# A new order for all engines in a windowed-attention and feed-forward kernel

## The chip, the cores and the metric

The kernel runs on one core of one Trainium2 chip. The metric is the device time of one execution in microseconds (us). Before the change it is 201.78 us, the median of 3 runs (201.47 to 201.82).

## What is computed

```
scores = q @ k.T / 8 - slope[h] * distance          # 4 batches, 8 heads, 768 positions, head size 64
keep   = (key < 8) | (0 <= query - key < 96)        # 8 global keys and a window of 96
a      = softmax(where(keep, scores, -1e9))
x      = (a @ v) laid out as 3072 tokens x 512
h      = x @ w_in                                   # 512 x 2048
out    = (h - tanh(h)) @ w_out                      # 2048 x 512, float32
```

## The kernel before

The 3072 tokens are cut into 24 blocks of 128 (numbered u = 0 to 23; blocks 0 to 3 are the first of each batch). A block needs only its own keys, those of the block before it, and the 8 global keys, which stand in the first block of its batch. Everything runs in one program without loops on the chip: the text `ORDER` lists some 970 steps by name, and at its end the kernel walks through the list and issues each step on its engine (lines 799 to 806). An engine executes its own steps in this order and waits, where a step needs another engine's result or a buffer that is still read; so the list is the schedule. `/a`, `/d`, `/p`, `/s` behind a name choose ScalarE (ACT), VectorE (DVE), GpSimd (POOL) or SyncE (SP) for a step that more than one engine can do. A second text, `HOMES`, says for each tile which buffer or PSUM bank it lives in; a wait for a free buffer comes from there.

The steps by name, with their lines in the profile:

- `lq.u`, `lk.u`, `lv.u` load a block's queries, keys and values (128 KB each as bfloat16). From block 4 on they are DMAs that POOL issues (L342), cast on the way; `in.j` and `out.j` (L345, L348) load the two weight matrices the same way.
- `T.u` transposes queries and keys. For blocks 0 to 6 the matrix engine (PE) does it, and `Te` copies the result out of PSUM; from block 7 on `T.u` is one DMA transpose that SP issues (L377). `K.u` and `V.u` copy the 8 global keys and values in.
- `S.n` computes scores on PE (L396), `E.u.o` the exponential on ACT (L403), `M` multiplies by the mask on DVE (L407, L412), `AV.u` multiplies by the values on PE (L427), `R` and `N` divide (L433, L444; L440 if ACT divides).
- `X.u` and `Xe.u` bring the block into transposed form; from block 8 on `Xe.u` is a DMA transpose on SP (L466).
- `m1.g.f` multiplies a group of blocks by pieces of w_in on PE (L477), `th` takes tanh on ACT (L576), `g` the difference on DVE (L590). Groups 0 and 1 are single blocks, 2 to 6 pairs, 7 to 9 fours. In groups 8 and 9 most of this is done by Strassen's scheme (`v`, `y`, `d`, `e`, `q`; L536 on PE).
- The second product is done in pairs of blocks by Strassen's scheme: `w` and `n` are sums on DVE (L617, L630), `p1` to `p7` the products on PE (L645), `a0` to `a2` copies and `c11` to `c22` the results (L274, L276, L659). `st` stores a block, issued by POOL or SP (L662).

Line 274 is the helper that copies on ACT, line 276 the one that copies on DVE. The steps that matter most below are these two, of which every line is as it was:

```
    def load_natural(e, dst, src, u):
        eng(e).dma_start(out=dst, in_=rows_of(src, u).rearrange("h p d -> p h d"))
...
    def a_DT(u):
        nc.sync.dma_start_transpose(
            out=buf(("qk", u)).rearrange("p a b f -> p (a b) f"), in_=buf(("kq", u)).rearrange("p a f -> p (a f)")
        )
```

and the walk through the list is

```
        for word in ORDER.split():
...
            name, _, side = word.partition("/")
            e, fn = acts[name]
            fn({"a": ACT, "d": DVE, "p": POOL, "s": SP}[side] if e is None else e)
```

Of the kernel before, what the change touches and what calls it, by code (L numbers as in the profile page):

```python
# [42 lines left out]
AV.13 K.15/d lq.18 n2.8/d a0.8/a m1.6.14 E.14.1 c11.8 lv.15 v2.3 m1.6.4 R.13 K.14/d th.6.14 N.13/d lv.16 p6.8 g.6.14
Xe.13 th.6.4 lq.19 g.6.4 S.13 a1.8/a M.14 p5.8 E.15.1 n4.8/d m1.6.0 E.16.0 T.18 M.15 m1.6.12 a2.8/a th.6.0 T.17 m1.6.8
E.16.1 g.6.0 AV.14 n3.8/d th.6.12 Xe.12 m1.6.10 th.6.8 V.14/d R.14 g.6.12 K.16/a AV.15 g.6.8 m1.6.2 N.14/d p7.8 R.15
th.6.2 N.15/d th.6.10 m1.6.6 c22.8 Xe.15 g.6.2 p4.8 th.6.6 g.6.10 Xe.14 g.6.6 p3.8 c21.8 p1.10 n1.10/d st.9.0/p c12.8/a
T.19 v1.2 lv.17 S.14 n2.10/d a0.10/a V.15/a M.16 lq.20 p2.10 E.17.1 lq.23 p6.10 n4.10/d E.18.0 lv.19 AV.16 a1.10/d
# [795 lines left out]
```

## Time and profile before

| what | value |
|---|---|
| median of 3 runs | 201.78 us |
| span of the profiled execution, first to last instruction | 199.8 us |
| median less span: what lies around the span | 1.98 us |
| PE busy | 193.1 us (97%) |
| DVE busy | 178.6 us (89%) |
| ACT busy | 135.1 us (68%) |
| POOL busy (it issues DMAs) | 75.3 us (38%) |

The span is that of one execution under the profiler; no separate time of that execution is given, so its own time is taken as its span and the 1.98 us around it. The page's second part cuts the span into 40 slices of 5 us and gives the busy share of each engine in tenths, the granted clock of PE, and the mean busy share of the 16 DMA engines. The queries used are the timeline (instructions of one engine in order of time: start, duration, line, what it wrote from what, and in brackets the idle time before it and what ended that), the groups of instructions by line, and the DMA issues (how many, their size, and the median time from issue to landing).

### The profile page before, as it was taken

What the parts mean: (1) busy time and instruction counts of PE and PEld (TensorE: products, weight loads), DVE (VectorE), ACT (ScalarE), POOL (GpSimd) and SP (SyncE); (2) the same over time, 40 slices, a digit from 0 to 9 for tenths busy, and PEclk for the clock granted to TensorE, in tenths of its full rate; (3) what the DMA queues carried; (4) which work ended last, traced back from release to release, by engine and by line L of the source; (5) the groups of instructions that cost most, each with busy time, mean ns of one, the idle gap of its engine ahead of it and who ended that gap; (6) DMA issues with size and microseconds to landing.
All of it is one profiled execution on the core that took longest, in us unless ns stands there. A gap on an engine that the chain in (4) does not pass through costs nothing.

```text
span 199.8 us, 5524 instructions
## 1 busy us (share of the span) xinstructions
PE 193.1 (97%) x2219; PEld 157.8 (79%) x2219; DVE 178.6 (89%) x348; ACT 135.1 (68%) x234; POOL 75.3 (38%) x97
## 2 busy tenths in 40 slices
PE   8799999999999999999999999999999999999992
...
PEclk9999999999999999999999999999999999999999
DMA  5999999999999999989996998994733101001233
GB/s 148 211 180 185 198 163 207 201 156 141 193 167 196 178 153 135 133 188 171 137 158 146 140 173 192 154 155 85 55 108 121 66 0 54 3 0 52 107 132 131
DMA packets 103545, 27.36 MB, mean 137 GB/s; under 512 B 93920, under 2 KB 101472, under 8 KB 103520
## 3 DMA queue, kind: packets, MB, share of 16 engines
q0 software_dynamic: 74048, 16.78, 89.5%
...
## 4 chain that ended last, share of the span: by engine, by line
PE 85%; DVE 7%; DMA 3%; ACT 2%; issue 1%; ACTq 0%; DVEq 0%
PE ps L645 36%; PE ps L477 27%; PE ps L536 9%; PE ps L396 5%; PE ps L427 5%; DMA f<-in_q_dram 3%; DVE gall L590 2%; DVE x L444 2%; DVE mem L407 1%; PE ps L455 1%; ACT mem L403 1%; PE ps L320 1%; ACT mem L274 1%; PE ps L365 1%; ACT th L576 1%
## 5 line engine op out<-in xcount | busy, mean ns | idle before, releaser
L477 PE MATMUL ps<-xT,w_in_bf 128*128 128x256 bf16 (+2 forms) x544 | 69.0, 279 | 0.0
L477 PEld LDWEIGHTS <-w_in_bf 128*128 128x128 bf16 x544 | 47.2, 98 | 12.4
L576 ACT ACTIVATE th<-ps 128x512 f32<-128x512 f32 (+1 forms) x74 | 41.8, 591 | 18.7 <-PE ps L477 13.6
L590 DVE TENSOR_TENSOR gall<-ps,th 128x512 bf16<-128x512 f32 (+1 forms) x74 | 47.4, 668 | 6.0 <-ACT th L576 5.6
L645 PEld LDWEIGHTS <-gall 128*128 128x128 bf16 x488 | 46.4, 98 | 7.0
L662 POOL DMA_DIRECT2D out_dram<-ot x14 | 8.1, 580 | 102.5 <-ACT ot L274 52.4
L403 ACT ACTIVATE mem<-ps 128x1024 bf16<-128x1024 f32 x44 | 43.3, 1024 | 4.3 <-PE ps L396 4.2
L645 PE MATMUL ps<-w_out_bf,gall 128*128 128x256 bf16 (+1 forms) x296 | 36.3, 270 | 0.0
L274 ACT COPY sn<-ps 128x256 f32<-128x256 f32 x32 | 12.0, 375 | 20.3 <-PE ps L645 16.3
L645 PE MATMUL ps<-f,ss 128*128 128x256 bf16 x192 | 24.9, 273 | 0.0
L645 PE MATMUL ps<-wc,gall 128*128 128x256 bf16 x192 | 24.9, 273 | 0.0
L342 POOL DMA_DIRECT2D vb<-in_v_dram x24 | 21.5, 900 | 2.2 <-issue 1.0
L645 PEld LDWEIGHTS <-ss 128*128 128x128 bf16 x192 | 18.3, 98 | 2.8
L342 POOL DMA_DIRECT2D mem<-in_k_dram x20 | 17.9, 899 | 4.8 <-DMA w_out_bf<-in_moe_w_out_dram 3.1
L342 POOL DMA_DIRECT2D mem<-in_q_dram x20 | 18.1, 904 | 3.8 <-DMA w_out_bf<-in_moe_w_out_dram 3.0
L412 DVE TENSOR_TENSOR mem<-mem,mk 128x2048 bf16<-128x2048 bf16 x16 | 19.2, 1215 | 0.0
L659 DVE TENSOR_TENSOR ot<-ps,sn 128x256 f32<-128x256 f32 x36 | 14.7, 415 | 3.6 <-ACT sn L274 2.5
L444 DVE TENSOR_TENSOR x<-ps,rden 128x512 bf16<-128x512 f32 x23 | 15.8, 687 | 0.5
L274 ACT COPY mem<-ps 128x512 f32<-128x512 f32 (+1 forms) x22 | 12.7, 585 | 5.1 <-PE ps L536 3.9
L427 PEld LDWEIGHTS <-mem 128*128 128x128 bf16 x352 | 13.4, 97 | 2.1 <-ACT mem L403 0.5
L427 PE MATMUL ps<-vb,mem 128*128 128x65 bf16 x352 | 14.7, 193 | 0.0
L396 PE MATMUL ps<-mem 64*128 64x128 bf16 x352 | 13.1, 217 | 0.0
...
## 6 DMA issues: line engine op xcount, KB each, us to landing
out_dram<-ot POOLq DMA_DIRECT2D x14, 256.0 KB, 2.8
vb<-in_v_dram POOLq DMA_DIRECT2D x24, 128.0 KB, 6.2
mem<-in_q_dram POOLq DMA_DIRECT2D x22, 128.0 KB, 6.3
mem<-in_k_dram POOLq DMA_DIRECT2D x22, 128.0 KB, 6.1
out_dram<-ot SPq DMA_DIRECT2D x9, 256.0 KB, 2.0
w_out_bf<-in_moe_w_out_dram POOLq DMA_DIRECT2D x4, 512.0 KB, 10.7
w_in_bf<-in_moe_w_in_dram POOLq DMA_DIRECT2D x4, 256.0 KB, 7.6
w_in_bf<-in_moe_w_in_dram POOLq DMA_DIRECT2D x2, 512.0 KB, 11.0
```

The source lines that it names most:

```text
L274: nc.scalar.copy(out=out, in_=in_)
L342: eng(e).dma_start(out=dst, in_=rows_of(src, u).rearrange("h p d -> p h d"))
L396: nc.tensor.matmul(bank(("s", u, o), hh)[:, p * P : (p + 1) * P], buf(("qk", back[u] if o else u))[r, 1, p, :], buf(("qk", u))[r, 0, p, :] ...
L403: nc.scalar.activation(d, banks(("s", u, o), 0, 1), AF.Exp, bias=0.0, scale=scale)
L412: nc.vector.tensor_tensor(out=t, in0=t, in1=mk[:, 1:3], op=ALU.mult)
L427: nc.tensor.matmul(t[:, h // (H // 2), h % (H // 2), :], buf(("p", u, o))[:, slot(h), :], buf(("v", back[u] if o else u))[:, h, 0 : Dh + 1 ...
L444: nc.vector.tensor_tensor(out=buf(("x", u)).rearrange("q (a h) d -> q a h d", a=2), in0=t[:, :, :, 0:Dh], in1=rden.to_broadcast([P, 2, H / ...
L477: nc.tensor.matmul(t[:, (f - f0) * n : (f - f0 + 1) * n], w_in_bf[j][:, c, fo : fo + P], x[:, c, 0:n], start=(c == 0), stop=(c == CD - 1),)
L536: nc.tensor.matmul(t[:, r * 2 * P : (r + 1) * 2 * P], w(r)[:, c], x[:, c], start=first and r + c == 0, stop=c == 1, skip_group_check=not f ...
L576: nc.scalar.activation(h_view(buf(("th", g, f0)), g, m), h_view(bank(("h", g, f0)), g, m), AF.Tanh, bias=0.0, scale=1.0)
L590: nc.vector.tensor_tensor(out=o, in0=v(h), in1=v(th), op=ALU.subtract)
L645: nc.tensor.matmul(bank((holder, a))[:, c0:c1], s(f), t(f)[:, c0:c1], start=first and f == 0, stop=f == HF - 1, skip_group_check=not first,)
```

## The change

Every step is kept. The order of the list, the engine of 49 copies, divisions and stores, and nearly all places in `HOMES` are replaced; no function is changed. Per engine, PE's steps keep their number and shape. Of the steps that several engines can do, 2 more of the 24 divisions (`N`) and one half of the last `c12` go to ACT, one `c12`, 3 of the 36 copies `a` and 3 of the 16 copies `K` go to DVE, and 3 stores go from POOL to SP (net). The loads keep their engine, but POOL issues them in another order: up to `out.3` the order is as before, past it it isn't, and SP's transposes stand in another order from T.11 on.

The lists, cut to the opening, the stretch from `out.3` to `AV.10`, and the end:

```
-lq.1 lk.1 zero rel ones.0 zero:7 dist lq.2 lq.0 lk.0 zero:7 zero:7 table lq.3 turn zero:7 first zero:7 lk.3 ident slopes
-zero:7 zero:7 lk.2 ones.1 B.0 lv.1 cq.1/a ck.1/d bm.1 lv.0 T.1.1 em.1 lv.2 T.1.0 Te.1.1/d B.1 cq.0/a lv.3 Te.1.0/d
-ck.0/a T.0.0 S.1 in.0 Te.0.0/a T.3.0 B.2 E.1.0 in.1 Te.3.0/d T.0.1 Te.0.1/d in.3 T.2.1 T.3.1 Te.2.1/a T.2.0 Te.3.1/d S.0
-lq.4 Te.2.0/a AV.1 E.0.0 S.2 R.1 N.1/d in.2 B.3 E.2.0 lk.4 AV.0 S.3 R.0 N.0/d X.1 in.4 E.3.0 AV.2 Xe.1/d X.0 in.5 R.2
-N.2/d bm.2 Xe.0/a AV.3 m1.1.0 lk.5 em.2 R.3 N.3/d X.2 m1.0.0 th.1.0 Xe.2/d X.3 lq.5 th.0.0 g.1.0 m1.0.2 Xe.3/a g.0.0
...
-th.1.8 M.4.0 E.4.1 m1.0.8 g.1.8 th.2.8 out.0 M.4.1 m1.0.12 th.0.8 g.2.4 out.2 T.5.1 g.2.8 T.5.0 Te.5.1/a m1.1.12 out.3
-Te.5.0/d th.0.12 g.0.8 S.5 lk.7 th.1.12 g.0.12 AV.4 E.5.0 g.1.12 lq.7 m1.2.12 n1.0/d E.5.1 lk.10 m1.2.10 M.5.0 lq.10
-V.4/a R.4 m1.2.14 M.5.1 th.2.10 K.5/d N.4/d AV.5 th.2.14 T.6.1 X.4 R.5 Te.6.1/a T.6.0 N.5/d lq.9 Xe.4/a Te.6.0/d X.5 S.6
-Xe.5/d g.2.14 m1.3.2 E.6.1 n3.0/d m1.3.10 g.2.10 lq.8 th.2.12 w1.1 th.3.2 p1.0 E.6.0 w1.0 m1.3.12 g.2.12 a0.0/a g.3.2
-m1.3.4 lk.8 th.3.12 n2.0/d K.6/a th.3.10 m1.3.0 w2.0 m1.3.8 w4.0 w2.1 lk.9 p2.0 M.6.0 p6.0 lv.7 g.3.12 w3.1 T.7 m1.3.6
-lv.6 a1.0/a c11.0 th.3.0 w3.0 p5.0 g.3.10 p7.0 a2.0/a n1.2/d th.3.4 g.3.0 p1.2 th.3.6 n2.2/d p2.2 a0.2/a w4.1 th.3.8
-c22.0 p6.2 V.5/a n4.2/d T.8 p4.0 n3.2/d a1.2/a g.3.8 T.9 p5.2 g.3.6 p7.2 c21.0 a2.2/a T.10 g.3.4 st.1.0/p p3.2 M.6.1
-lk.11 c11.2 S.7 c12.2/a c22.2 lv.11 n4.0/d AV.6 E.7.1 p4.2 lk.12 R.6 N.6/d E.7.0 m1.3.14 lv.9 K.7/d V.6/d M.7.1 X.6
-lk.16 th.3.14 p3.0 M.7.0 Xe.6/a c21.2 lq.11 AV.7 g.3.14 c12.0/a lk.13 R.7 S.8 N.7/d lq.12 n1.4/d X.7 E.8.1 p1.4 Xe.7/d
-lv.10 n2.4/d m1.4.8 K.9/a E.8.0 v1.1 st.2.0/p n3.4/d m1.4.10 th.4.8 a0.4/d lv.8 g.4.8 p6.4 th.4.10 v2.1 E.9.0 lq.13
-m1.4.14 g.4.10 M.8 a1.4/a S.9 th.4.14 T.11 p5.4 g.4.14 E.9.1 V.7/d p2.4 a2.4/d E.10.0 M.9 T.12 m1.4.2 E.10.1 n4.4/d
-m1.4.6 K.10/a st.0.0/s M.10 AV.9 th.4.6 m1.4.0 th.4.2 g.4.6 m1.4.4 R.9 T.13 N.9/d p7.4 g.4.2 th.4.4 Xe.9 th.4.0 g.4.4
-AV.8 V.9/a p3.4 c11.4 c22.4 R.8 m1.4.12 N.8/d c12.4/a st.4.0/p g.4.0 p4.4 Xe.8 th.4.12 lq.15 v3.1 S.10 c21.4 lk.15
-g.4.12 p1.6 E.12.0 lv.13 n1.6/d p2.6 n2.6/d a0.6/a lq.14 E.11.1 K.12/d AV.10 lk.14 p6.6 E.11.0 R.10 c11.6 V.10/d lq.16
...
-c11.18 a2.20/a st.19.0/s n2.22/d c12.18/a p1.22 st.18.0/s c22.20 c11.20 p4.20 a0.22/a c11.22 p6.22 n4.22/d st.22.0/s
-c21.20 p7.22 a1.22/a st.21.0/p p5.22 p3.20 a2.22/a c22.22 p3.22.0 c12.20/a p4.22 st.20.0/s c12.22.0/d st.22.256/s
-p3.22.1 c21.22 c12.22.1/d st.23.0/s st.22.384/s
...
+lq.1 lk.1 zero rel ones.0 zero:7 dist lq.2 lq.0 lk.0 zero:7 zero:7 table lq.3 turn zero:7 first zero:7 lk.3 ident
+slopes zero:7 zero:7 lk.2 ones.1 B.0 lv.1 cq.1/a ck.1/d bm.1 lv.0 T.1.1 em.1 lv.2 T.1.0 Te.1.1/d B.1 cq.0/a T.2.0 lv.3
+Te.1.0/d ck.0/a T.0.0 S.1 in.0 T.0.1 Te.0.0/a T.3.0 Te.2.0/d T.3.1 in.1 Te.0.1/d T.2.1 S.0 Te.2.1/d E.1.0 B.2 S.2 AV.1
+in.3 Te.3.1/a E.0.0 AV.0 Te.3.0/a R.1 E.2.0 R.0 N.1/d B.3 S.3 AV.2 X.1 lq.4 in.2 N.0/d lk.4 in.4 R.2 N.2/d X.0 Xe.1/d
+bm.2 E.3.0 AV.3 X.2 Xe.0/a m1.0.0 m1.1.0 em.2 R.3 N.3/d X.3 m1.0.2 m1.1.2 th.0.0 Xe.3/a Xe.2/d in.5 lk.5 m1.2.2 th.2.2
...
+Te.5.1/a S.5 th.0.12 g.0.12 g.1.8 out.3 m1.2.14 lk.8 th.1.12 g.1.12 AV.4 m1.2.10 E.5.1 T.6.1 M.5.1 T.6.0 E.5.0 R.4
+M.5.0 lq.7 lq.8 V.4/a AV.5 N.4/d X.4 Te.6.1/a th.2.10 m1.2.12 R.5 K.5/d Te.6.0/a N.5/d X.5 Xe.4/a S.6 n1.0/d Xe.5/d
+m1.3.2 th.2.14 g.2.14 th.2.12 E.6.0 m1.3.8 m1.3.10 m1.3.6 lk.7 T.7 g.2.12 w1.1 g.2.10 th.3.2 g.3.2 V.5/a n3.0/d n1.2/d
+m1.3.0 th.3.6 E.6.1 w3.0 p1.2 a0.2/a p1.0 a0.0/a m1.3.4 n2.2/d th.3.4 p2.0 w1.0 w2.0 w2.1 w4.1 p6.2 n2.0/d p6.0 th.3.10
+a1.2/a p5.2 a1.0/a M.6.1 T.8 g.3.6 g.3.10 w3.1 c11.0 g.3.4 p2.2 n4.2/d c11.2 p7.0 p5.0 th.3.8 a2.2/a lq.9 lv.9 th.3.0
+K.6/a p3.2 m1.3.12 a2.0/a w4.0 g.3.8 c22.0 th.3.12 c12.2/a lv.6 lk.9 T.9 p4.0 n3.2/d g.3.0 p7.2 M.6.0 AV.6 V.6/a g.3.12
+c21.0 S.7 lk.10 E.7.0 c22.2 p4.2 R.6 N.6/d m1.3.14 X.6 lq.10 T.10 E.7.1 K.7/d n4.0/d p3.0 c21.2 M.7.0 lv.20 lv.7 M.7.1
+AV.7 lk.12 lk.14 th.3.14 g.3.14 Xe.6/a c12.0/a S.8 lq.19 st.1.0/p R.7 N.7/d V.7/a lk.13 X.7 p1.4 lq.12 Xe.7/d n1.4/d
+n2.4/d a0.4/d E.8.1 E.9.0 m1.4.14 E.8.0 T.12 th.4.14 g.4.14 m1.4.10 th.4.10 K.9/d g.4.10 m1.4.8 th.4.8 p6.4 a1.4/a S.9
+E.9.1 g.4.8 M.8 E.10.0 lv.8 p5.4 M.9 a2.4/a m1.4.6 th.4.6 E.10.1 lk.11 lq.11 AV.8 m1.4.12 n3.4/d th.4.12 m1.4.4 T.11
+R.8 N.8/d g.4.6 v1.2 AV.9 R.9 th.4.4 g.4.4 g.4.12 lk.16 st.0.0/p st.2.0/s v2.1 lv.14 Xe.8 st.3.0/p p2.4 c11.4 m1.4.2
+N.9/a Xe.9 m1.4.0 lv.11 n4.4/d lq.13 T.13 lq.17 th.4.2 g.4.2 th.4.0 g.4.0 v3.2 p7.4 p3.4 K.10/a S.10 c22.4 M.10 V.9/d
+c12.4/a n1.6/d lk.19 lk.18 lv.13 n2.6/d p1.6 p4.4 lq.15 lk.15 lv.10 E.11.1 E.12.0 K.11/d c21.4 a0.6/d K.12/d p2.6 c11.6
+lq.14 lv.21 lq.16 n3.6/d AV.10 lq.23 V.10/a R.10 E.11.0 m1.5.10 th.5.10 N.10/d p6.6 a1.6/a st.5.0/s Xe.10 S.11 v4.1
...
+a1.20/a n4.22/d c11.22 p6.22 a1.22/a c21.18 p5.20 c12.18/a st.18.0/s st.17.0/s p5.22 st.19.0/p n3.22/d p7.22 n3.20/d
+st.22.0/s p7.20 a2.22/a c22.22 p4.22 a2.20/a c22.20 n4.20/d c21.22 p4.20 c21.20 st.21.0/s p3.20 c12.20/a c11.20
+st.20.0/s st.23.0/p p3.22.0 c12.22.0/a st.22.256/s p3.22.1 c12.22.1/d st.22.384/s
```

`HOMES` (the first line of each):

```
-v.0:1 tr.0.1:6 tr.0.0:6 kq.0:2 qk.0:6 v.1:0 tr.1.1:6 tr.1.0:7 kq.1:0 qk.1:5 v.2:2 tr.2.1:7 tr.2.0:5 kq.2:1 qk.2:8 v.3:3
...
+v.0:1 tr.0.1:7 tr.0.0:6 kq.0:2 qk.0:0 v.1:0 tr.1.1:6 tr.1.0:7 kq.1:0 qk.1:5 v.2:2 tr.2.1:6 tr.2.0:2 kq.2:1 qk.2:4 v.3:3
...
```

More of the change, by code (lines that the diff above doesn't have):

```diff
@@ L43 @@
[L43 to L47, printed above, removed]
@@ new lines @@
+lq.14 lv.21 lq.16 n3.6/d AV.10 lq.23 V.10/a R.10 E.11.0 m1.5.10 th.5.10 N.10/d p6.6 a1.6/a st.5.0/s Xe.10 S.11 v4.1
+g.5.10 M.11 E.12.1 M.12 E.13.1 p5.6 m1.5.8 AV.11 th.5.8 E.13.0 T.15 lk.20 lv.12 lv.19 m1.5.12 R.11 g.5.8 th.5.12 m1.5.6
+lk.21 th.5.6 p7.6 m1.5.0 th.5.0 V.11/a T.16 T.14 m1.5.2 a2.6/d M.13 N.11/d g.5.12 m1.5.14 g.5.6 n4.6/d AV.12 p3.6
+th.5.2 th.5.14 g.5.0 R.12 c22.6 p4.6 N.12/d V.12/a c12.6/d g.5.2 c21.6 m1.5.4 S.12 g.5.14 lv.22 lk.17 lv.23 th.5.4
+g.5.4 n1.8/d p2.8 E.14.0 K.15/d n2.8/d p1.8 E.15.0 AV.13 R.13 N.13/d E.14.1 T.19 Xe.11 m1.6.4 m1.6.14 th.6.4 T.17 Xe.12
@@ new lines @@
+a0.8/d c11.8 th.6.14 K.14/d g.6.4 p6.8 a1.8/a g.6.14 M.14 n3.8/d S.13 v2.2 v4.2 E.15.1 M.15 E.16.0 E.16.1 m1.6.10
+th.6.10 p5.8 m1.6.12 th.6.12 AV.14 m1.6.6 m1.6.2 R.14 N.14/d n4.8/d V.14/a th.6.6 th.6.2 g.6.12 lv.15 lq.18 lv.17
+st.4.0/s AV.15 V.15/a m1.6.8 m1.6.0 g.6.6 R.15 N.15/d g.6.2 g.6.10 p7.8 th.6.8 a2.8/a th.6.0 p3.8 T.18 Xe.13 v1.3 c22.8
+p4.8 g.6.8 g.6.0 n1.10/d K.16/a c12.8/a S.14 E.17.0 K.17/a E.18.0 st.6.0/p lv.16 c21.8 n2.10/d Xe.14 p1.10 a0.10/d
+p2.10 Xe.15 n4.10/d c11.10 p6.10 E.17.1 a1.10/d m1.7.2 th.7.2 st.9.0/p lv.18 p5.10 a2.10/a M.16 S.15 E.19.1 E.19.0
@@ new lines @@
+n3.12/d c21.10 n2.12/d AV.18 R.18 N.18/d p2.12 E.20.0 V.19/d n1.14/d lk.23 T.23 a0.12/a p6.12 c11.12 E.21.0 S.17
+n4.12/d Xe.17 a1.12/a p5.12 E.22.1 p7.12 a2.12/a p3.12 M.20 AV.20 n2.14/d c22.12 K.22/d p4.12 E.21.1 M.21 V.20/d E.22.0
+c12.12/a Xe.18 Xe.16 R.20 S.18 E.23.1 E.23.0 p2.14 N.20/d AV.21 c21.12 st.13.0/p M.22 p1.14 d2.8.1 V.21/d AV.22 d1.8.1
+a0.14/a p6.14 R.21 M.23 y1.8 V.22/d N.21/a AV.23 y2.8 R.22 N.22/d e0.8.1/a d6.8.1 e1.8.1/a q11.8.1 c11.14 Xe.20 R.23
+m1.8.0 d5.8.1 e2.8.1/a th.8.0 N.23/d a1.14/d y4.8 g.8.0 d1.8.2 d2.8.3 e0.8.2/a d3.8.1 th.8.4 d2.8.2 q11.8.2 y3.8 p5.14
@@ new lines @@
+d6.8.2 a2.14/a d7.8.1 e1.8.2/a g.8.4 d1.8.3 e0.8.3/a Xe.21 Xe.22 q22.8.1 st.11.0/s d5.8.2 m1.8.1 e2.8.2/a n3.14/d
+q11.8.3 n4.14/d th.8.1 d6.8.3 g.8.1 Xe.23 y1.9 d3.8.2 m1.8.3 e1.8.3/a th.8.3 d4.8.1 th.8.8 y3.9 d5.8.3 q21.8.1 g.8.3
+y2.9 p3.14 e2.8.3/a c12.14/a d7.8.2 d1.9.2 e0.9.2/a g.8.8 d3.8.3 th.8.12 q22.8.2 d7.8.3 q22.8.3 d6.9.2 e1.9.2/a p7.14
+th.8.6 d4.8.3 g.8.12 d4.8.2 d5.9.2 q21.8.3 q21.8.2 g.8.6 d2.9.2 q11.9.2 e2.9.2/a m1.9.2 d3.9.2 d1.9.1 m1.8.2 th.9.2
+th.8.14 m1.9.0 e0.9.1/a d6.9.1 c22.14 g.9.2 th.8.2 g.8.14 g.8.2 th.9.0 g.9.0 th.8.10 g.8.10 d2.9.1 p4.14 c21.14 m1.9.1
```

126 lines of the change are left out of this document (56 added, 70 removed).

## Prediction

> **What bounds the kernel now.** I read the page first, then the matrix engine's (PE's) timeline for gaps, then POOL's and SP's timelines with the DMA issues, because both end in DMA. From the page:
>
> ```profile
> span 199.8 us, 5524 instructions
> PE 193.1 (97%) x2219; PEld 157.8 (79%) x2219; DVE 178.6 (89%) x348; ACT 135.1 (68%) x234; POOL 75.3 (38%) x97
> PE   8799999999999999999999999999999999999992
> PEclk9999999999999999999999999999999999999999
> DMA  5999999999999999989996998994733101001233
> q0 software_dynamic: 74048, 16.78, 89.5%
> PE 85%; DVE 7%; DMA 3%; ACT 2%; issue 1%; ACTq 0%; DVEq 0%
> ```
>
> PE is busy throughout at full granted clock and carries 85% of the chain that ended last. The reader should also see the DMA row: nine tenths and more in nearly every 5 us slice up to about 130 us. There are two full resources; whoever reorders the second can stop the first. The PE timeline shows where PE now stands still (brackets) and two places used below:
>
> ```profile
> 1.00 3.17 PE L795 MATMUL ps<-zero 128*128 128x512 bf16 x7 [1.00 <-DVE vb L316]
> 3.96 1.91 PE L320 MATMUL ps<-slopes,dist 128*128 128x512 bf16 x4
> 8.44 0.40 PE L361 MATMUL ps<-turn,mem 128*128 128x128 bf16 x4 [1.21 <-ACT mem L274]
> 14.33 0.40 PE L455 MATMUL ps<-ident,x 128*128 128x128 bf16 x4 [0.18 <-DVE x L444]
> 34.52 0.40 PE L455 MATMUL ps<-ident,x 128*128 128x128 bf16 x4 [0.38 <-DVE x L444]
> 56.13 0.65 PE L427 MATMUL ps<-vb,mem 128*128 128x65 bf16 x16
> 57.85 0.40 PE L455 MATMUL ps<-ident,x 128*128 128x128 bf16 x4 [0.30 <-DVE x L444]
> 75.67 0.65 PE L427 MATMUL ps<-vb,mem 128*128 128x65 bf16 x16
> ```
>
> Past the warm-up, PE waits 1.21 + 0.18 + 0.38 + 0.30 = 2.07 us in all, and not at all after 58 us. The steps are the same in number and shape, so this 2.07 us is all that an order of engines can win on PE. Row 56.13 is AV.7, row 75.67 is AV.10 (the two calls of L427 with 16 products that stand there in the list).
>
> **Part 1: PE, DVE, ACT.** Counted off both lists, PE's steps ahead of AV.7, S.8, S.9, AV.10, S.11 and S.12 are the same sets before and after; only their order inside changes. So without waits AV.10 comes where it came, 75.67, less what is recovered. T.2.0 moves into the gap at 8.44, but that gap waits for ACT's cast of q, and the same casts and exponentials follow it on ACT; I count 0.3 of the 1.21 + 0.18 as won, and the 0.38 and 0.30 as gone because other products now stand ahead of those transposes: 1.0 us in all, at most 2.07, at least 0 (what is late next is always a DVE result; DVE is 89% busy). Side changes: two of 24 divisions (N) leave DVE for ACT net, from
>
> ```profile
> L444 DVE TENSOR_TENSOR x<-ps,rden 128x512 bf16<-128x512 f32 x23 | 15.8, 687 | 0.5
> L440 ACT ACTIVATE x<-ps,rden 128x64 bf16<-128x64 f32 x8 | 1.8, 330 | 0.5 <-DVE rden L433 0.5
> ```
>
> that is 2 x 0.69 us off DVE and 2 x 1.8 us onto ACT, which is idle a third of the time; three small `a` copies and three K copies go to DVE in return. I take nought; uncovered, it is at most 2 x (1.8 - 0.7) = 2.2 us, if every such N stood on the path. The end:
>
> ```profile
> 195.60 0.61 PE L645 MATMUL ps<-w_out_bf,gall 128*128 128x128 bf16 x8
> 196.24 0.29 DVE L276 COPY ot<-ps 128x128 f32<-128x128 f32 x1
> ```
>
> The last copy starts as the last product ends (196.21) although c21.22 stood ahead of it on DVE; the new list has that product, copy and 64 KB store last too. Nought. Swapping stores between POOL and SP moves work between issuers only.
>
> **Part 2: what POOL and SP are moved past.** This is the part that costs. After the fourth piece of w_out (out.3), POOL's list was lk.7 lq.7 lk.10 lq.10 lq.9 lq.8 lk.8 lk.9 lv.7 lv.6, st.1, lk.11 lv.11 lk.12 lv.9 lk.16 lq.11 lk.13 lq.12 lv.10: the values of block 10 are the 19th load behind the weights. Now it is lk.8 lq.7 lq.8 lk.7 lq.9 lv.9 lv.6 lk.9 lk.10 lq.10 lv.20 lv.7 lk.12 lk.14 lq.19, st.1, lk.13 lq.12 lv.8 lk.11 lq.11 lk.16, st.0, lv.14, st.3, lv.11 lq.13 lq.17 lk.19 lk.18 lv.13 lq.15 lk.15 lv.10: lv.10 is the 31st. Twelve loads have been put ahead of it: lv.8 and lq.13, due about then, and ten that nobody reads before S.12 (lk.14 lq.15 lk.15 for S.12; lv.20 lq.19 lv.14 lq.17 lk.19 lk.18 lv.13 for later blocks); AV.10 needs it at the same place as before. PE issues in order, so everything behind AV.10 waits with it.
>
> When can the 31st land? First, loads with nothing beside them. POOL's timeline gives issues (start, us; idle before), the DMA issues of the same instants the time to landing (last column):
>
> ```profile
> 25.95 2.24 POOL L348 DMA_DIRECT2D w_out_bf<-in_moe_w_out_dram  x3 [1.99 <-DMA w_in_bf<-in_moe_w_in_dram]
> 33.36 0.88 POOL L342 DMA_DIRECT2D mem<-in_q_dram  x1 [1.03 <-DMA w_out_bf<-in_moe_w_out_dram]
> 41.00 0.88 POOL L342 DMA_DIRECT2D mem<-in_k_dram  x1 [1.31 <-DMA w_out_bf<-in_moe_w_out_dram]
> 43.43 0.88 POOL L342 DMA_DIRECT2D vb<-in_v_dram  x1 [0.47 <-DMA mem<-in_k_dram]
> 51.27 0.58 POOL L662 DMA_DIRECT2D out_dram<-ot  x1 [6.97 <-DVE ot L659]
> ```
>
> ```profile
> w_out_bf<-in_moe_w_out_dram POOLq DMA_DIRECT2D x1, 512.0 KB, 13.3
> mem<-in_q_dram POOLq DMA_DIRECT2D x1, 128.0 KB, 11.6
> mem<-in_k_dram POOLq DMA_DIRECT2D x1, 128.0 KB, 6.5
> vb<-in_v_dram POOLq DMA_DIRECT2D x1, 128.0 KB, 8.1
> ```
>
> out.3, third of the row at 25.95, is issued at 25.95 + 2.24 - 0.75 = 27.4 and lands at 27.4 + 13.3 = 40.7. lq.9 lands at 33.36 + 11.6 = 45.0, lk.9, three loads later, at 41.00 + 6.5 = 47.5: 0.85 us a load. The queue is full: POOL's waits at 33.36, 41.00 and 43.43 end with a landing. Second, loads beside SP's DMA transposes. SP's timeline, then the landings:
>
> ```profile
> 46.73 1.52 SPq L377 DMA_TRANSPOSE mem<-mem  x1
> 63.82 1.92 SPq L377 DMA_TRANSPOSE mem<-mem  x1
> 98.97 3.01 SPq L377 DMA_TRANSPOSE mem<-mem  x1
> 97.57 1.23 SPq L377 DMA_TRANSPOSE mem<-mem  x1
> 59.02 0.94 POOL L342 DMA_DIRECT2D vb<-in_v_dram  x1
> 59.88 0.65 POOL L662 DMA_DIRECT2D out_dram<-ot  x1
> ```
>
> ```profile
> mem<-mem SPq DMA_TRANSPOSE x1, 5.5
> mem<-mem SPq DMA_TRANSPOSE x1, 5.6
> mem<-mem SPq DMA_TRANSPOSE x1, 5.1
> mem<-mem SPq DMA_TRANSPOSE x1, 5.7
> vb<-in_v_dram POOLq DMA_DIRECT2D x1, 128.0 KB, 5.4
> out_dram<-ot POOLq DMA_DIRECT2D x1, 256.0 KB, 5.2
> ```
>
> The landings stand in the order of the issues. Between lk.9 (47.5) and T.8 (46.73 + 5.5 = 52.2) land two loads and T.7, T.8: (4.7 - 1.7) / 2 = 1.5 us of queue time for each transpose. Between lv.10 (59.02 + 5.4 = 64.4) and T.12 (63.82 + 5.6 = 69.4) land the store st.2 (59.88 + 5.2 = 65.1, so 0.7), two loads and T.11, T.12: (5.0 - 0.7 - 1.7) / 2 = 1.3. With no load beside it T.17 (98.97 + 5.1 = 104.1) follows T.18 (97.57 + 5.7 = 103.3) by 0.8. So a transpose costs 0.8 to 1.5 us of DMA; I take 1.3, since 59 to 69 us is the stretch most like the new one.
>
> The sum: 40.7 + 31 loads x 0.85 = 26.35 + T.7 to T.12 and the half-sized Xe.8 and Xe.9, 7 x 1.3 = 9.1, + four stores (st.1, st.0, st.3, and st.2 on SP) x 0.7 = 2.8 gives 79.0 us; with 0.8 it is 75.5, with 1.5 it is 80.4. If DMA never limits, POOL's own pace does: its store st.1 cannot go out before its data (51.3 in the old order); from there 15 more loads x 0.88 and 3 stores x 0.58 lead to an issue near 66 to 67 and, with 5.4 to land, 72.
>
> So AV.10 waits until about 79.0 instead of starting at 75.67 less 1.0: PE stands still for some 4.3 us, and the end moves by 79.0 - 75.67 = 3.3 us. What was won earlier is swallowed, since the wait ends with a landing. Behind it the loads that went early are in place, so nothing else should be late; the next DMA chain, T.14 to T.16 into S.12, has 12 us. Earlier, lv.7 is the 12th load: 40.7 + 10.2 + 2 to 3 transposes x 1.3 is 53.5 to 54.8, against 56.13 - 1.0; it just fits. Span 199.8 + 3.3 = 203.1; around the span lie 201.78 - 199.8 = 1.98 us of the median of the runs, and the profiled execution has no other time of its own, so I keep that: **205.1 us**.
>
> The Trainium skill, "DMA: Bandwidth & Descriptors", section "Issuing engines are not separate DMA queues", says that transfers started by SP, ACT and POOL run on the same 16 DMA engines and interleave. The trace agrees (1.3 to 1.5 us for a transpose beside loads, 0.8 alone), and the rule speaks against this change: if the queues were separate, lv.10 would land at 40.7 + 26.35 + 2.1 = 69 us by DMA and nothing would wait.
>
> **Rivals.** *A, DMA keeps up: faster.* If a transpose costs 0.8 us or less beside loads, lv.10 lands by 75.5, AV.10 hardly waits, and the gaps recovered remain: 201.78 - 1.0 = 200.8 us. The turning point is a price of (75.6 - 40.7 - 26.35 - 2.8) / 7 = 0.82 us. For it: T.17 behind T.18. Against it: both stretches with loads.
>
> *B, a draw.* lv.10 lands between 74.7 and 76, or small DVE waits in new places take the 1.0 us back: 201.4 to 202.2 us. For it: DVE's 89%; against: it needs two effects to cancel.
>
> *C, PE is slow after its wait.* The 512-wide products at 1.00 to 3.96 us start 2.96 / 7 = 0.42 us apart and those of the next row (3.96) hold about 1.9 us for four, whereas at 8.44 us four 128-wide ones, as many columns as one of these, have ended 0.40 us after their start with their pipeline's tail: PE began at about half pace for some 4.6 us. A stop of 4.3 us may bring that state back; if it does for as long, 4.6 / 2 = 2.3 us are lost: 207.4 us. It decides only if the wait is one piece. Against it: after the 1.21 us gap nothing slowed, and no longer gap exists to look at. The Trainium skill, "TensorE: Matmul & The Clock Gate", Part 1, states that the array falls to half clock after an idle window of about 3.4 us; no run here shows it.
>
> **How the numbers follow.** About 0.2% (0.4 us) is what a measurement of this kernel can tell from no change. Chances: forecast (203 to 206.6 us, prices 1.1 to 1.5) 0.60; C 0.13; A 0.17; B 0.10, of which 0.06 lies within 0.2% and the rest splits evenly. Faster 0.19, same 0.06, slower 0.75. The range must reach into A on one side and C on the other: 200.7 to 207.6; the forecast's own range is 203.0 to 206.6.
>
> **What would show it.** In the new profile: one long PE gap (3 to 5 us) ahead of a 16-product L427 row near 75 us, released by the DMA of `vb<-in_v_dram`; loads issued on POOL without a pause from 51 to 68 us, with landing times of 8 us and more; SP transposes at 6 to 8 us; no DMA left of loads after about 120 us; PE gaps elsewhere under 0.5 us each. Wrong if lv.10 is landed before PE asks for it, if the gap stands at an S (then a transpose, not a load, is late), or if PE's gaps are many and end with DVE.

## The result and the profile after

The changed kernel takes 216.25 us, the median of 6 runs (214.78 to 216.97), against 201.87 us (201.47 to 202.66) for the kernel before beside it: 1.07 times as long, 95% interval 1.067 to 1.073. The profiled execution took 216.97 us with a span of 215.2 us. The forecast was 205.1 us and its range ended at 207.6: slower was right, the size was not. Times below are medians of all executions of a kernel, while the ratios leave out executions in the chip's slower state, so the two need not agree to the last digit. The page after (span, slices of PE, granted clock, DMA, and the engines' shares of the chain that ended last):

```profile
span 215.2 us, 5522 instructions
PE   7798999998869954899999999999999999999993
PEclk9999999999978999589999999999999999999999
DMA  6999999999999999999995299822332201000144
PE 53%; DMA 33%; POOL 8%; issue 2%; ACT 1%; DVE 1%; DVEq 0%; POOLq 0%; SPq 0%
```

Two things changed against the page before. PE has holes between 48 and 92 us, and its clock falls behind two of them (59 to 70 and 86 to 97 us), while DMA is at nine tenths in every slice there: DMA stands on the chain with 33% where it had 3%. And DMA is ahead of its old course: its row drops to 5 and 2 between 113 and 124 us, where it stood at eight and nine until 135 us in every slice but one, and the last load lands at 132.4 us, 142.1 before. The new kernel moves the same bytes sooner, and PE waits meanwhile. PE's timeline has the waits (brackets: idle before, and what ended it):

```profile
53.61 0.62 PE L396 MATMUL ps<-mem 64*128 64x128 bf16 x16 [0.79 <-DMA mem<-mem]
60.81 0.40 PE L396 MATMUL ps<-mem 64*128 64x128 bf16 x8 [2.56 <-DMA mem<-mem]
62.24 4.45 PE L477 MATMUL ps<-xT,w_in_bf 128*128 128x256 bf16 x24
77.84 1.03 PE L645 MATMUL ps<-wc,gall 128*128 128x256 bf16 x8 [2.31 <-DVE ot L659]
87.06 1.04 PE L427 MATMUL ps<-vb,mem 128*128 128x65 bf16 x16 [3.81 <-DMA vb<-in_v_dram]
87.91 1.90 PE L477 MATMUL ps<-xT,w_in_bf 128*128 128x256 bf16 x8
89.60 1.91 PE L645 MATMUL ps<-f,ss 128*128 128x256 bf16 x8
91.44 1.46 PE L396 MATMUL ps<-mem 64*128 64x128 bf16 x24
93.78 1.04 PE L477 MATMUL ps<-xT,w_in_bf 128*128 128x256 bf16 x8
204.52 1.03 PE L645 MATMUL ps<-f,ss 128*128 128x256 bf16 x8 [0.41 <-ACT sn L274]
208.67 1.03 PE L645 MATMUL ps<-wc,gall 128*128 128x256 bf16 x8 [0.27 <-DVE ot L659]
211.37 0.61 PE L645 MATMUL ps<-w_out_bf,gall 128*128 128x128 bf16 x8 [0.35 <-ACT ot L274]
```

In order: S.7 (53.61) waits for T.7, which lands at 53.6 us, and the last third of S.8 (60.81) for T.9, which lands at 60.8; p7.4 (77.84) waits for DVE, whose result waits for a buffer; AV.10 (87.06) waits for lv.10, as forecast. (The expectations below call the third one p3.4, which is the product next to it.) Behind two of the waits PE is slow: eight products of 256 columns take 1.90 and 1.91 us at 87.91 and 89.60, the same kind 1.04 at 93.78. At 62.24 the 24 take 4.45 us; 24 of the same kind take 2.78 at 97.76. The clock of those stretches (the granted clock, PEclk, is the last number but two: 0.73 and 0.62):

```profile
60.00:65.00 5.00, 4.19 (x34) 3.19 (x35) 2.22 (x5) 2.54 (x3) 2.90 (x4) 0.73 2.93 131
85.00:90.00 5.00, 2.94 (x26) 2.33 (x27) 1.23 (x3) 1.69 (x3) 1.41 (x2) 0.62 2.29 178
```

The sum: waits 0.79 + 2.56 + 2.31 + 3.81 = 9.5; slow products (4.45 - 2.78) + 0.4 (AV.10: 1.04 for 0.65) + 0.9 + 0.9 + 0.6 (91.44: 1.46 for 0.84) = 4.5; waits at the end 0.41 + 0.27 + 0.35 = 1.0. Together 15.0 of the 15.4 us that the span grew.

What p7.4 waits for stands in the timeline of DVE, that of SP, and the DMA issue of that instant (last column: us to landing):

```profile
77.37 0.42 DVE L659 TENSOR_TENSOR ot<-ps,sn 128x256 f32<-128x256 f32 x1 [2.59 <-DMA out_dram<-ot]
```

```profile
64.40 5.38 SPq L377 DMA_TRANSPOSE mem<-mem  x2
69.88 0.53 SPq L662 DMA_DIRECT2D out_dram<-ot  x1
```

```profile
out_dram<-ot SPq DMA_DIRECT2D x1, 256.0 KB, 7.4
```

The store of block 2, whose data were complete near 52 us, stands on SP behind T.12 and T.11, whose loads landed late; it is issued at 69.88, lands at 77.3, and only then can DVE write the next result into that buffer and free the PSUM bank that p7.4 writes. That bank is new: in `HOMES` the result that c11.4 reads (q.4) and the one that p7.4 writes (z.4) now share bank 2, where they had banks 0 and 3. Last, the load of lv.10 on POOL's timeline, and its DMA issue:

```profile
74.70 0.88 POOL L342 DMA_DIRECT2D vb<-in_v_dram  x1 [1.11 <-DMA vb<-in_v_dram]
```

```profile
vb<-in_v_dram POOLq DMA_DIRECT2D x1, 128.0 KB, 12.2
```

It lands at 74.7 + 12.2 = 86.9 us; the forecast was 79.0.

### The profile page after: what moved, and what is told of

Same layout as the page of the kernel before. It is cut to its first block, busy times and chain, and to the rows that moved or that the text cites. A ratio compares the mean times of both kernels' runs of the same rounds, so it can differ in the third digit from the quotient of the medians.

```text
span 215.2 us, 5522 instructions
## 1 busy us (share of the span) xinstructions
PE 197.0 (92%) x2210; PEld 159.5 (74%) x2219; DVE 179.3 (83%) x352; ACT 138.1 (64%) x244; POOL 73.5 (34%) x94
## 4 chain that ended last, share of the span: by engine, by line
PE 53%; DMA 33%; POOL 8%; issue 2%; ACT 1%; DVE 1%; DVEq 0%; POOLq 0%; SPq 0%
PE ps L645 22%; PE ps L477 16%; DMA mem<-in_k_dram 10%; DMA vb<-in_v_dram 10%; PE ps L536 8%; DMA w_in_bf<-in_moe_w_in_dram 6%; DMA mem<-mem 4%; PE ps L427 3%; PE ps L396 3%; DMA out_dram<-ot 3%; POOL mem L342 2%; POOL w_in_bf L345 2%; POOL vb L342 2%; POOL mem L339 1%; POOL w_out_bf L348 1%
## 5 line engine op out<-in xcount | busy, mean ns | idle before, releaser
L477 PE MATMUL ps<-xT,w_in_bf 128*128 128x256 bf16 (+2 forms) x537 | 70.9, 284 | 1.2 <-DMA w_in_bf<-in_moe_w_in_dram 0.9
L477 PEld LDWEIGHTS <-w_in_bf 128*128 128x128 bf16 x544 | 48.3, 100 | 15.0 <-DMA w_in_bf<-in_moe_w_in_dram 1.1
L662 POOL DMA_DIRECT2D out_dram<-ot x11 | 6.3, 572 | 99.1 <-DVE ot L659 97.4
L645 PE MATMUL ps<-wc,gall 128*128 128x256 bf16 x192 | 24.4, 272 | 2.6 <-DVE ot L659 2.6
L645 PEld LDWEIGHTS <-ss 128*128 128x128 bf16 x192 | 18.8, 100 | 4.0 <-issue 1.0
L274 ACT COPY sn<-ps 128x256 f32<-128x256 f32 x29 | 10.7, 372 | 15.6 <-PE ps L645 11.0
L396 PE MATMUL ps<-mem 64*128 64x128 bf16 x352 | 14.0, 223 | 3.6 <-DMA mem<-mem 3.4
L396 PEld LDWEIGHTS <-mem 64*128 64x128 bf16 x352 | 10.5, 97 | 7.5 <-DMA mem<-mem 3.6
```

Of the source, the lines that this page charges most:

```text
L274: nc.scalar.copy(out=out, in_=in_)
L396: nc.tensor.matmul(bank(("s", u, o), hh)[:, p * P : (p + 1) * P], buf(("qk", back[u] if o else u))[r, 1, p, :], buf(("qk", u))[r, 0, p, :] ...
L477: nc.tensor.matmul(t[:, (f - f0) * n : (f - f0 + 1) * n], w_in_bf[j][:, c, fo : fo + P], x[:, c, 0:n], start=(c == 0), stop=(c == CD - 1),)
L645: nc.tensor.matmul(bank((holder, a))[:, c0:c1], s(f), t(f)[:, c0:c1], start=first and f == 0, stop=f == HF - 1, skip_group_check=not first,)
```

## The experiments

Theory Q says that loads put ahead of due ones in a full DMA queue cost all of it; O that the new order of PE, DVE and ACT costs by itself; R, formed on the way, that it is how far POOL runs ahead. Ratios are against the kernel before, measured beside each run.

**1. The ten early loads behind lv.10** (`late_ten`):

```diff
-... lv.20 lv.7 ... lk.14 lq.19 ... lv.14 ... lq.17 ... lk.19 lk.18 lv.13 ... lq.15 lk.15 lv.10 ... lq.14 lv.21 lq.16
+... lv.7 ... lv.10 lq.15 lk.15 lk.14 ... lq.14 lv.21 lq.16 lv.13 lv.14 lq.17 lk.18 lk.19 lq.19 lv.20
```

> The changed kernel with ten loads that nobody reads before S.12 (lv.20, lk.14, lq.19, lv.14, lq.17, lk.19, lk.18, lv.13, lq.15, lk.15) issued behind lv.10 instead of ahead of it; all else as in the changed kernel. Theory Q (the early loads fill the shared DMA queue; every wait of PE between 52 and 90 us comes of it): lv.10 lands ten loads earlier, at about 75 instead of 86.9 us, and the waits at S.8 (2.56 us), p3.4 (2.31) and AV.10 (3.81) and the slow products behind them (1.5 and 2.8 us) go, 13.0 us in all: 203.3 us, between 201.5 and 206. Theory O (the new order of PE, DVE and ACT is what costs, the loads are only where it shows): the waits come back with other releasers, 211 us or more.

Measured: 216.28 us, ratio 1.062 (1.048 to 1.076). Q missed: lv.10 lands at 71.8 us and AV.10 doesn't wait, but nothing is won. O's 211 us and more, with other releasers, is met in size, but what PE now waits for are transfers again, so it isn't shown that the order of the engines costs. In a trace of 217.69 us PE's waits over 0.9 us past 50 us are now

```profile
77.70 1.87 PE L645 MATMUL ps<-wc,gall 128*128 128x256 bf16 x8 [5.64 <-DVE ot L659]
103.21 1.46 PE L396 MATMUL ps<-mem 64*128 64x128 bf16 x24 [4.32 <-DMA mem<-mem]
```

that is 5.64 us for the same store (DVE's row stands still until it lands) and 4.32 us at S.12 for a transpose, each followed by slow products.

**2. lv.10 alone moved up** (`lv10_up`): `lv.10` from ahead of `E.11.1` to ahead of `lv.20`.

> The changed kernel with lv.10 alone moved up, ahead of lv.20; the ten early loads stay. The recorded prediction (only lv.10 is late, nothing behind it): the wait at AV.10 and the slow products behind it go and nothing takes their place, 216.2 - 3.8 - 2.8 = 209.6 us. Theory Q (everything in the queue is late): T.13, which landed at 85.7 us, is next; S.11 wants it 2.2 us of products behind AV.10, near 85.4 us, and T.13 moves one load later, so S.11 waits 1 to 2 us: 210.5 to 212 us.

Measured: 215.97 us, ratio 1.061 (1.048 to 1.074). AV.10's wait is gone, as both expected; the wait that grew is again the store's, before PE ever comes to AV.10 or S.11:

```profile
80.52 1.86 PE L645 MATMUL ps<-wc,gall 128*128 128x256 bf16 x8 [6.65 <-DVE ot L659]
```

**3. The store of block 2 earlier** (`store_first`): `st.2.0/s` from behind `T.11` to ahead of `T.12`.

> The changed kernel with the store of block 2 on SP moved ahead of T.12 instead of behind T.11. If the wait of 2.31 us ahead of p3.4 comes from that store (its buffer), the wait goes. Theory Q: the wait at AV.10 ends with lv.10's landing at 86.9 us, which doesn't move, so it grows by what was won, from 3.8 to about 6 us, and the time stays at 216.2 us, at most 0.5 us less. If the two waits were independent terms: 216.2 - 2.3 = 213.9 us.

Measured: 215.07 us, ratio 1.062 (1.051 to 1.072). The wait of p7.4 is gone, lv.10 lands at 86.0 us (86.9 in the changed kernel), and what was won is swallowed there but for 1.2 us, where Q allowed 0.5; that is less than the spread of its executions (214.67 to 216.78):

```profile
86.14 1.04 PE L427 MATMUL ps<-vb,mem 128*128 128x65 bf16 x16 [5.41 <-DMA vb<-in_v_dram]
```

**4. Both edits** (`late_ten_store`).

> The changed kernel with both single edits: the ten loads behind lv.10 and the store of block 2 ahead of T.12 on SP. Alone each left the time at about 215 to 216 us. Theory Q: the wait for the store's buffer (5.6 us in the first) and that at AV.10 (5.4 us in the second) both go, but the ten loads still stand ahead of much that S.12 needs (lq.14, T.13, T.14 behind Xe.10 on SP), so that part of the lateness comes back as one wait at S.12: 208 to 212 us. If the two waits were all: 216.2 - 13 = 203 us.

Measured: 216.65 us, ratio 1.074 (1.070 to 1.079). S.10 and AV.10 come at 73.3 and 76.7 us, near the kernel before (73.1 and 75.7); then AV.12 stands still for lv.12, which is now behind the seven moved loads:

```profile
98.36 1.06 PE L427 MATMUL ps<-vb,mem 128*128 128x65 bf16 x16 [9.19 <-DMA vb<-in_v_dram]
```

Four edits, four times the same end: each moves the wait to the next transfer that is late. Not even the size of one wait can be read as what it is worth.

**5. Products in the waits** (`warm`): ten `zero:2` ahead of S.8, sixteen `zero:3` ahead of AV.10.

> The changed kernel with products of zeros in the waits: 10 of 512 columns ahead of S.8 and 16 ahead of AV.10, into the bank that the waiting step writes next; 2.1 and 3.4 us of work at full clock, less than the waits. If the clock falls because PE stands still: it stays at 1.00 behind both waits. What is won behind S.8 (1.5 us) is swallowed by the wait ahead of p3.4, which ends with a landing; what is won behind AV.10 (2.8 us) stays: 213.5 us. If the slow products have another cause (operands, contention with DMA), they stay slow: 216.2 us.

Measured: 219.4 us, ratio 1.079 (1.065 to 1.092). On the clock it gives the answer: with PE kept busy, the 24 products behind S.8 and the eight behind AV.10 run at full speed.

```profile
57.89 2.32 PE L796 MATMUL ps<-zero 128*128 128x512 bf16 x10
62.50 2.78 PE L478 MATMUL ps<-xT,w_in_bf 128*128 128x256 bf16 x24
85.84 3.62 PE L796 MATMUL ps<-zero 128*128 128x512 bf16 x16
89.78 1.03 PE L478 MATMUL ps<-xT,w_in_bf 128*128 128x256 bf16 x8
```

So standing still is what slows them. As a gain it missed: what S.8 won made the store's wait longer (4.86 us), PE came to AV.10 only at 85.8, and the sixteen products outlasted lv.10's landing (86.9) by 2.4 us.

**6. Copies in place of transposes** (`plain_copy`; queries and keys are not transposed):

```diff
-        nc.sync.dma_start_transpose(
-            out=buf(("qk", u)).rearrange("p a b f -> p (a b) f"), ...
+        nc.sync.dma_start(
+            out=buf(("qk", u)).rearrange("p a b f -> p (a b f)"), ...
```

> The changed kernel with the 17 DMA transposes of queries and keys on SP replaced by plain DMA copies of the same 256 KB between the same buffers (the transposition is left out; Xe stays a DMA transpose). If a transpose beside loads costs about 2.3 us of DMA time (what the 45.4 us between out.3 and lv.10 leave over for each of the seven), a copy of 0.7 to 1 us brings lv.10 in 6 us and more earlier, at 77 to 81 us: 206 to 210 us. If the loads themselves are slower than 0.85 us there and the transposes are not the cost, lv.10 lands where it did and the time stays at 215 to 217 us.

Measured: 209.2 us, ratio 1.033 (1.026 to 1.040); lv.10 lands at 80.7 us, both inside what was expected if the transposes are the cost.

```profile
80.84 0.64 PE L427 MATMUL ps<-vb,mem 128*128 128x65 bf16 x16 [2.90 <-DMA vb<-in_v_dram]
```

The prediction and this expectation left a transfer out: T.13 too lands ahead of lv.10 (85.7 us in the changed kernel), so seven whole transposes and two half ones, eight in all, stand there. With loads at 0.85 and stores at 0.7 as in the prediction, each has (86.9 - 41.5 - 26.35 - 2.8) / 8 = 2.0 us; in this kernel, where out.3 lands at 40.8, (80.7 - 40.8 - 26.35 - 2.8) / 8 = 1.3, with the two Xe still transposes. These prices are what the sum leaves over, not measured one by one. Without the transposition lv.10 lands 6.2 us earlier, of which out.3 gives 0.7; the rest goes with the transposition.

**7. All transfers in the order of need** (`due_order`; PE, DVE, ACT and all places as changed). The part that matters, with each engine's list written by itself:

```diff
+POOL: lq.7 lk.7 lk.8 lq.8 lq.9 lk.9 lv.6 lk.10 lq.10 lv.7 lk.12 lq.12 lk.11 lq.11 lv.8 lv.9 lk.13 lq.13 st.1 lv.10 st.0 lv.11
+      lk.14 lq.15 lk.15 lq.14 lk.16 lq.16 lq.19 lk.19 st.3 lv.12 lv.13 lk.18 lq.18 lq.17 lk.17 lv.14 lv.15 st.6 ...
+SP:   T.7 T.8 T.9 T.10 T.12 st.2 T.11 T.13 Xe.8 Xe.9 T.15 T.14 Xe.10 st.5 T.16 T.19 ...
```

> The changed kernel, its order of PE, DVE and ACT and all places of tiles untouched; past out.3 the loads and stores of POOL and the transposes and stores of SP are put in the order in which PE would need them if it never waited (each about 12 us ahead of its reader, or when its buffer or data come free). Theory Q (all of the loss is DMA work in the wrong order; DMA is full, so whatever goes early makes something due late): PE's waits past 50 us fall below 1.5 us in all and the time comes to 202 to 204.5 us. Theory O (the new order of PE, DVE and ACT costs by itself): 208 us or more, with waits that end with DVE or ACT.

**8. The ten loads put back into that order** (`due_early_ten`).

> due_order with the ten loads that nobody reads before S.12 put back ahead of lv.10 (lv.20 behind lv.7, lk.14 and lq.19 behind lk.12, the other seven behind st.0). Theory Q: 10 x 0.85 us of transfers and more go ahead of lv.10, T.13 and the loads behind them; the lateness of 8 to 10 us comes back at AV.10 or the S behind it: 210 to 214 us. If the ten loads are not what costs (as the kernel with only them moved back suggests, 216.3 us), it stays within 1.5 us of due_order.

Measured: 212.95 us, ratio 1.053 (1.048 to 1.059), and 213.16 us, ratio 1.056 (1.052 to 1.060). Order is worth 3 us of 14, and the ten loads, by themselves, nothing that can be measured; only the place of the longest wait differs, Xe.9 in the first, lv.10 in the second:

```profile
80.33 1.87 PE L477 MATMUL ps<-xT,w_in_bf 128*128 128x256 bf16 x8 [3.61 <-DMA xT<-x]
```

```profile
84.30 1.04 PE L427 MATMUL ps<-vb,mem 128*128 128x65 bf16 x16 [6.06 <-DMA vb<-in_v_dram]
```

Q has fallen as it was stated, and O's 208 us and more is met in size, but the longest waits end with DMA, not with DVE or ACT. What `due_order` has in common with the changed kernel is shown by the DMA issues between 50 and 90 us (last column: median us from issue to landing), of the kernel before, the changed one, `due_order` and, ahead of its time, the next experiment:

```profile
vb<-in_v_dram POOLq DMA_DIRECT2D x6, 128.0 KB, 5.2
mem<-mem SPq DMA_TRANSPOSE x8, 5.5
```

```profile
vb<-in_v_dram POOLq DMA_DIRECT2D x7, 128.0 KB, 9.4
mem<-mem SPq DMA_TRANSPOSE x6, 9.6
```

```profile
vb<-in_v_dram POOLq DMA_DIRECT2D x7, 128.0 KB, 8.7
mem<-mem SPq DMA_TRANSPOSE x8, 8.8
```

```profile
vb<-in_v_dram POOLq DMA_DIRECT2D x9, 128.0 KB, 6.4
mem<-mem SPq DMA_TRANSPOSE x8, 7.5
```

Before, POOL issued nothing between lq.13 and st.4:

```profile
61.33 0.96 POOL L342 DMA_DIRECT2D mem<-in_q_dram  x1
72.15 0.58 POOL L662 DMA_DIRECT2D out_dram<-ot  x1 [9.87 <-ACT ot L274]
```

st.4 waited for its data, and the five loads behind it (lq.15 lk.15 lv.13 lq.14 lk.14) for buffers that AV.8 frees at 70.6 us. From 68.5 us, when the last load had landed, until 72.15 transposes and stores had DMA to themselves. With the new places four of these five loads find their buffer free 16 us and more earlier; from 55.1 to 74.7 us POOL never pauses for over 1.2 us. Counted from issues and landings between 50 and 90 us, POOL had 2.9 transfers under way on average before, 6.7 in the changed kernel and in `due_order`, and 4.5 in the next experiment. In none of the traces are there ever more than eight: with eight under way, POOL issues the next when one lands, as after its pause of 1.11 us at 74.70.

**9. POOL held back** (`paced`): as 7, with the loads put behind steps for which POOL has to wait.

```diff
-... lv.7 lk.12 lq.12 lk.11 lq.11 lv.8 lv.9 lk.13 lq.13 st.1 lv.10 st.0 lv.11 lk.14 lq.15 lk.15 lq.14 lk.16 lq.16 lq.19 lk.19 st.3 lv.12 lv.13 ...
+... lv.7 st.1 lk.12 lq.12 lk.11 lq.11 lv.9 lv.8 lk.13 lq.13 lv.10 lv.11 lk.16 st.0 lv.13 lq.15 lk.15 st.4 lq.14 lk.14 lq.16 lv.12 st.3 st.5 lv.19 lk.19 lq.19 ...
-SP: ... T.10 T.12 st.2 T.11 ... Xe.10 st.5 T.16 ... st.4 ...
+SP: ... T.10 st.2 T.12 T.11 ... Xe.10 T.16 ...
```

> due_order with POOL held back: the loads stand behind steps for which POOL has to wait anyway (st.1 at 52 us, lv.13 until AV.8 has freed its buffer near 65 us, st.4 until its data near 75, lv.12 until AV.10, lv.19 until AV.11, lv.15, st.6, st.9), so that it issues nothing long ahead of its reader; st.2 goes on SP ahead of T.12; st.4 and st.5 move from SP to POOL. Orders of PE, DVE and ACT and all places are the changed kernel's. Theory R (not which load stands first, but how far POOL runs ahead: due_order's transfers took 8 to 15 us to land because 10 and more were under way, before's took 5): landings fall to 5 to 7 us, Xe.9 lands by 77 us instead of 80.2, PE's waits between 50 and 130 us fall below 1.5 us in all and the products stay at full clock; with the 1.2 us that the end lost, 203 to 205 us. Theory O (the new order of PE, DVE and ACT costs by itself): 208 us or more as due_order, with waits that end with DVE or ACT.

Measured: 206.24 us, ratio 1.016 (1.010 to 1.023), a little over R's 203 to 205 us: Xe.9 lands at 77.1 us as expected, but PE's waits between 50 and 130 us still add up to 2.6 us. POOL's holds in its timeline, the clock on the page, and the one wait of over 0.9 us that PE's timeline still has past 50 us:

```profile
65.14 0.89 POOL L342 DMA_DIRECT2D vb<-in_v_dram  x1 [2.22 <-PE ps L427]
72.17 0.58 POOL L662 DMA_DIRECT2D out_dram<-ot  x1 [4.39 <-ACT ot L274]
```

```profile
PEclk9999999999999999999999999999999999999999
```

```profile
77.22 1.03 PE L477 MATMUL ps<-xT,w_in_bf 128*128 128x256 bf16 x8 [1.76 <-DMA xT<-x]
```

With the same steps on PE, DVE and ACT in the same order, 10 of the 14.4 us are gone. How much goes ahead of need can be counted from the landings: of the 72 loads, so many had landed when S.12 started:

| kernel | S.12 starts | loads landed |
|---|---|---|
| before | 89.5 us | 48 |
| after | 103.6 us | 59 |
| late_ten | 103.2 us | 60 |
| due_order | 96.3 us | 55 |
| paced | 90.5 us | 50 |

S.12 needs the same blocks in each. The count by itself doesn't tell cause from effect, since DMA goes on while PE waits; run 9, which changes only the transfers, does.

**10. The old order at the end** (`paced_tail`): from `p5.20` on, PE, DVE and ACT as before the change.

> paced with the steps of PE, DVE and ACT from p5.20 on (the last two pairs of blocks) in the order that they had before the change. The end of the changed kernel loses about 1.2 us more than before's in waits of 0.2 to 0.6 us (p7.22, p4.20, p3.20, p3.22.1) that no load is near. If that is the order of those steps: 1.0 us less than paced. If not: the same as paced within 0.4 us.

Measured: 212.73 us, ratio 1.046 (1.039 to 1.053), which neither expectation allowed. Inconclusive: the stores kept the new order while the results came in the old one, so DVE stood 4.24 us for a store's buffer, and PE with it:

```profile
198.79 0.76 DVE L659 TENSOR_TENSOR ot<-ps,sn 128x256 f32<-128x256 f32 x2 [4.24 <-DMA out_dram<-ot]
```

```profile
199.27 3.57 PE L645 MATMUL ps<-wc,gall 128*128 128x256 bf16 x16 [3.95 <-DVE ot L659]
```

**11 and 12. The opening and the Xe** (`paced_open`: `T.2.0` from ahead of `T.0.0` to behind `T.0.1`, and `T.13` behind `Xe.9`; `paced_late15`: besides, `lq.15` and `lk.15` behind `st.4`).

> paced with two small edits: T.2.0 goes behind T.0.1 (in the changed kernel it stands ahead of T.0.0 and waits for the load of block 2's queries; m1.0.2 starts anywhere from 16.0 to 18.6 us in the traces so far), and SP issues T.13 behind Xe.8 and Xe.9 instead of ahead of them (paced still waits 1.86 us at m1.5.10 for Xe). If both waits come from those places: m1.0.2 near 16.0 us in every execution, no wait over 0.5 us at m1.5.10, 202.5 to 204 us, and a narrower spread of runs than paced's 204 to 208. If Xe is late because the DMA engines are full (its place on SP doesn't matter): the wait stays at 1.5 us or more, or comes back at S.11 as T.13, and the time at 204 to 206 us.

> paced_open with two more loads held back, lq.15 and lk.15, from AV.8 (65 us) to behind st.4 (75 us). Theory R: two transfers less under way while Xe.8, Xe.9 and T.13 move, 1.7 us of DMA: they land by 75.5 us and no wait is left there; T.15 and T.14 then land near 87 us, just ahead of S.12 (89.5): 0.5 to 1 us less than paced_open if that fits, 1 to 2 us more if S.12 waits.

Measured: 204.47 us, ratio 1.010 (1.007 to 1.013), and 210.14 us, ratio 1.037 (1.033 to 1.042). The opening came as expected: m1.0.2 starts at 16.0 and 15.9 us in these two, anywhere from 16.0 to 18.7 in the traces with T.2.0 ahead. The Xe, now issued ahead of T.13, are as late as before, so their place on SP isn't what delays them; that DMA is full is the expectation's other reading, and it fits:

```profile
77.75 1.03 PE L477 MATMUL ps<-xT,w_in_bf 128*128 128x256 bf16 x8 [2.31 <-DMA xT<-x]
96.11 1.91 PE L477 MATMUL ps<-xT,w_in_bf 128*128 128x256 bf16 x16 [1.89 <-DMA xT<-x]
```

Holding back two loads more takes the wait at m1.5.10 down to 0.6 us, as expected, and S.12 waits 0.6 us; but the next Xe is late by far more and the slow clock is back (in a trace of 211.24 us). The time is 5.7 us above `paced_open`, where 2 at most were expected:

```profile
98.34 3.57 PE L477 MATMUL ps<-xT,w_in_bf 128*128 128x256 bf16 x16 [5.17 <-DMA xT<-x]
```

No version beat the kernel before.

## Why the prediction was right and wrong

- **PE and DMA are both full; who reorders the second stops the first**: right, and more so than its sum.
- **lv.10 late, AV.10 stands still**: the step was right in its place (AV.10, released by `vb<-in_v_dram`, 3.81 us against 4.3), not in its time, so the near match of the wait is luck: PE came to AV.10 some 8 us later than forecast (83.3 for 74.7) just as lv.10 landed 7.9 later. The term that was mis-sized is the price of a transpose among loads: 1.3 us, taken from 59 to 69 us, became 2.0, and T.13 was left out of the count; 8 x 2.0 for 7 x 1.3 is most of the 7.9 us by which lv.10 came later.
- **One wait of PE, all others at nothing**: this is the step that failed, and with it the whole frame. The forecast is 4.3 - 1.0 = 3.3 us; the span grew by 15.4: AV.10's wait 3.8, three waits that stood at nothing 0.8 + 2.6 + 2.3 = 5.7, slow products 4.5, the end 1.0, and nothing recovered. The prediction followed one transfer through the queue and counted the transposes only as work ahead of lv.10; in a full queue T.7, T.9 and a store were late before it. Ahead of AV.10 it looked at lv.7 alone. "It just fits" held there: lv.7 lands at 55.8 us and AV.7 starts at 57.0 without a wait.
- **"Behind it nothing else should be late"**: in the changed kernel's own trace this holds, PE has no wait over 0.25 us between AV.10 and 204 us. But it holds because PE had lost so much by then: runs 1, 2 and 4 take the forecast's wait away and stay at 216.0 to 216.7 us, and in 1 and 4 a later step waits instead (S.12 4.32 us, AV.12 9.19). A budget was wanted: how much DMA work must be done by each step of PE, and how much is.
- **"Swapping stores between POOL and SP moves work between issuers only"**: failed. SP waits for T.12's and T.11's loads, and the store behind them frees a buffer: 2.31 us, 6.65 in run 2.
- **1.0 us recovered in the opening and at the transposes**: not seen in the sum. The waits at X.5 and X.7 are gone as counted (0.38 and 0.30 us), but PE waits in the opening for two loads, 0.80 us at T.2.0 for block 2's queries and 0.90 at m1.0.2 for a piece of w_in, and m1.3.2 starts at 35.58 us (35.50 before). In the other traces with this opening it starts between 34.7 and 37.1; with T.2.0 moved back at 34.7 and 34.5. A gain was there to be had, and hung on loads.
- **The end at nought**: 1.0 us of waits. Its cause within the order is open, since run 10 told nothing.
- **Changes of side at nought**: nothing in the runs speaks against it; `paced` has all of them but two stores.
- **Rival C, slow PE behind a wait**: it had 0.13 and came true twice, 1.7 and 2.8 us, where it was priced at 2.3. It was treated as another case, though the forecast's own wait was its condition: with a wait of 4 us it belonged in the sum.
- **The range and the signs**: prices of 1.1 to 1.5 give 203.7 to 206.5 us by the prediction's own sum, not 203 to 206.6. Of its signs the wait at AV.10 and landings of 8 us and more came (9.4); a sign of being wrong came too, waits at an S (0.79 and 2.56 us), and loads land up to 132.4 us, where nothing was expected after about 120.

Shown is that most of the loss is in the transfers: runs 9 and 11 keep the places and, but for one transposition in 11, the order of PE, DVE and ACT, and come within 1.6% and 1.0% of the kernel before. Shown too is that single edits don't carry it (1 to 4, 8). That run-ahead does more than order rests on 7 against 9, the count of transfers under way and the landing times; it isn't isolated, since 9 also moves three stores and reorders some loads, and holding back two loads more (12) made it worse. Open is what the last 2.6 us of `paced_open` need, whether any order of transfers serves this order of PE as well as the old one, and why a transpose costs more here than in the kernel before.
